# A three-stage kernel on one core: the first expert's routing, list and gather moved in the order of the work

## The chip, the cores and the metric

The kernel runs on one core of a Trainium2 chip, in one launch. The metric is the device time in microseconds (us). Five engines work side by side, each from its own queue in order: TensorE (PE), VectorE (DVE), ScalarE (ACT), GpSimd (POOL) and SyncE (SP, which only issues DMAs here). They meet at semaphores. An instruction that waits holds everything behind it in its queue.

## What is computed

Three stages, each fed by the one before, over N = 2304 tokens with 512 features:

```python
# 1 retention: 4 batches, 8 heads, 576 positions, head size 64
ret = scores * Dmat          # Dmat: gamma_h ** (i - j) for i >= j, else 0
x = (ret @ v) as [2304, 512]
# 2 experts: logits = x @ w_gate, [2304, 8]; the greedy assignment goes through
#   all (token, expert) pairs by falling logit, each expert takes 288 tokens at most
out[mask_e] = relu(x[mask_e] @ w1[e]) @ w2[e]      # w1: 512x1024, w2: 1024x512
# 3 gated layer: h = x @ w_in (512x2048); out = (h * tanh(softplus(h))) @ w_out
```

## The kernel before, in words

**Retention** (`attention`). The tokens are 18 tiles of 128. A loop over tiles issues loads, scaling, scores, the carried state, outputs and, one tile late, `turn`: it transposes the tile's result on TensorE, where the same matmuls give the eight logits of each token, sums these on DVE into `L` (L248) and stores the rows to `x_scratch` in HBM. The order on PE, DVE and POOL is the program's own.

**Routing** (`choices`, `reached`, `route`). The greedy assignment is done one expert at a time: find the expert that fills up first, and the threshold logit at which it does. `choices` makes, for each token, the best logit and its expert as a one-hot (five DVE instructions, L357 to L362, over a range of tiles). `reached` (L369) marks which of 63 thresholds a token's best logit reaches. TensorE sums these marks over all tokens into `pF`; DVE tests which experts are full (`sat`, L374), TensorE turns that into a digit (`pD`, L458). Six such steps (s = 0 to 5, L419 to L458) give the threshold. Then DVE marks the tokens over it and at it (`gt`, `eq`), counts them with scans and a matmul (`pP`, L482), and has each token's place in the expert's list (`pos`, L495 to L504). Two instructions (L501, L502) put the taken tokens into `dead`, and `widen` (L515, L516) closes the expert in `L` and in `open`, so that `choices` can be made for the next. In the kernel before, the first choices are made after the loop, in two batches: tiles 0 to 15, then 16 and 17.

**List, gather, weights.** `tokens` turns `pos` into a list: small DVE instructions (L579 to L589), two halves of one-hots (`ohb`, L595), two halves of nine matmuls on TensorE (`pI`, L603), a sum on DVE (`chosen`, L607). GpSimd then issues three indirect DMAs of 96 rows each (L615, `xg`), TensorE transposes the rows (L636), ACT and DVE split them into a rounded part and its remainder (`xh`, `xl`). `weights_of` reads the expert's number on SP (from `eid`, L533) and loads 8 units of 512 KB (L551; units 0 to 3 are w1, 4 to 7 are w2) into 5 stage buffers; ACT rounds each (`whi`, L565), POOL or DVE subtracts (`wlo`, L568). Each product is three matmuls (high by high, high by low, low by high): `mma` is the expert's first layer (8 outputs of 12 matmuls), `mmb` the second (L779).

**The planner** (`run_tasks`). From the routing on, the order on every engine is made when the program is built: each task is a generator that asks for an engine, a time in ns, the events it follows and a priority; the planner keeps a clock for each engine, adds a HOP of 200 between tasks, takes the task that can begin first, and holds one back if a more urgent one would begin before it ends. The lines of a task between two requests are issued when the request is granted. The planned times thus set only the order in each queue; on the chip each instruction waits for its semaphores. Costs that matter here: the sums after the marks 1600, a half of the list's matmuls 740, three gather issues 4900, the gather's landing `GATHER` = 10000 behind them, a weight unit's landing 2000 (`DMA_WAIT`) for units 0 and 1 and 8000 (`LATE`) for the others. Priorities: `eid` -2, the list -1, routing 0, products 2, weights 3; smaller is more urgent.

`warm` fills TensorE with matmuls on zeros (215 and a HOP each in the plan, L789) from the first list until expert 0's features are there. `narrow` starts once expert 0's first output is planned: it reads w_in and w_out (8-byte numbers), makes 4-byte numbers of them on ACT, DVE and POOL, and writes them back for the last stage; 32 pieces of 512 KB, the first three loaded by SP. `final_units` then loads them as units 64 to 79.

**Gated layer** (`tiles`, `hidden`, `gate`, `outer`): six tiles of 384 tokens, all weights kept in SBUF; the change doesn't touch it.

Of the kernel before, what the change touches and what calls it, by code (L numbers as in the profile page):

```python
# [13 lines left out]
ALU = mybir.AluOpType  # L14
# [7 lines left out]
E = 8  # L22
# [3 lines left out]
NT = N // P  # L26
HP = H // 2
WARM = 11
STRADDLE = (4, 13)

GB = 96
# [9 lines left out]
PE, DVE, POOL, ACT, SP = "pe", "dve", "pool", "act", "sp"  # L41
# [3 lines left out]
DMA_WAIT = 2000  # L45
LATE = 8000
GATHER = 10000
SCATTER = 3200
FIRST = 163
SECOND = 216  # L50
# [2 lines left out]
FIRST_UNITS = 2  # L53
# [75 lines left out]
class Kernel:  # L129
# [3 lines left out]
    def attention(self):  # L133
        tc, nc, a = self.tc, self.nc, self.a
# [7 lines left out]
        with ExitStack() as st:  # L142
# [130 lines left out]
            scale(0, nc.vector)  # L273
            scale(1, nc.gpsimd)
            scale(2, nc.gpsimd)
            for t in range(NT - 1):
                load(t + 3)
                scale(t + 3, nc.gpsimd)
                scores(t + 1)
                carried(t, Sb[seen[0] % 2])  # L280
                outputs(t)
                state(t)
                turn(t - 1)
                if t == 6:
                    self.routing_consts()
            t = NT - 1
            carried(t, Sb[seen[0] % 2])
            outputs(t)
            turn(t - 1)
            self.psum = lambda name, shape: ps.tile(shape, F32, name=name, tag="pS" if name == "pF" else "pA", bufs=1 if name == "pF" else 2)  # L290
            G = self.marks_of()
            self.chosen = self.rw.tile([GB, E, 3], I32, name="chosen", bufs=1)
            pF = self.psum("pF", [P, E])
            early, late = slice(0, t - 1), slice(t - 1, NT)
            choice = self.choices(early)
            self.reached(choice, G, early)
            turn(t)
            self.choices(late, choice)
            self.reached(choice, G, late)
# [49 lines left out]

    def choices(self, ts=slice(0, NT), into=None):  # L350

        pool, v, L = self.rw, self.nc.vector, self.L
# [6 lines left out]
        v.tensor_tensor(cand, L[:, ts], raw[:, :, None].to_broadcast(both), op=ALU.is_equal)  # L359
        v.tensor_tensor(cand, cand, self.rc[:, None, RC["prio"]].to_broadcast(both), op=ALU.mult)  # L360
        v.tensor_reduce(top, cand, AX.X, ALU.max)
        v.tensor_tensor(oh, cand, top[:, :, None].to_broadcast(both), op=ALU.is_equal)  # L362
        return into

    def reached(self, choice, G, ts):

# [10 lines left out]
    def route(self):  # L377
# [3 lines left out]
        tc, nc, L, rw = self.tc, self.nc, self.L, self.rw  # L381
        rc, ic, icp, v = self.rc, self.ic, self.at("ic", U32), self.nc.vector
        choice, sat = self.first_step
        at = Event(0)
        self.marks = set()
        for i in range(E):
# [102 lines left out]
            if i:  # L489
                self.widen(i, ohe)  # L490
                self.spawn(self.weights_of(junk, at, i))
                choice = yield from self.choose(i, at)
            at = yield DVE, 1600, [marked, at], 0
            pose = rw.tile([P, NT], F32, name="pose")
            v.scalar_tensor_tensor(pose, scan[:, 1], pP[:, 1:2], eq, op0=ALU.add, op1=ALU.mult)  # L495
            v.scalar_tensor_tensor(pos, scan[:, 0], pP[:, 0:1], gt, op0=ALU.add, op1=ALU.mult)
            fin = self.at("fin")
            v.scalar_tensor_tensor(fin, pose, CAP + 0.5, eq, op0=ALU.is_lt, op1=ALU.mult)
            if i == 0:
                self.spawn(self.weights_of(junk, at, i))  # L500
            v.tensor_tensor(self.dead, self.dead, gt, op=ALU.add)  # L501
            v.tensor_tensor(self.dead, self.dead, fin, op=ALU.add)  # L502
            v.tensor_tensor(pose, pose, fin, op=ALU.mult)
            v.tensor_tensor(pos, pos, pose, op=ALU.add)  # L504
            self.spawn(self.tokens(i, pos, at))
            if i == 0:
                at = yield DVE, 300, [at], 0
                self.widen(i, ohe)
                choice = yield from self.choose(i, at)

# [7 lines left out]
    def choose(self, i, at):  # L518
        if i == E - 2:
            return None  # L520
        yield DVE, 1750, [at], 0
        return self.choices()

    def weights_of(self, junk, at, i):

        nc, a, rw = self.nc, self.a, self.rw
        units = {}
        self.weights.append(units)
        n0 = len(self.weights) * 8 - 8
        at = yield DVE, 160, [at], EID  # L530
        eid = rw.tile([P, 1], I32, name="eid")
        with nc.allow_low_precision(reason="small integers"):
            nc.vector.tensor_reduce(eid, junk, AX.X, ALU.add)  # L533
        at = yield SP, 1000, [at, *([lambda: self.loaded.get(n0 - 1)] if n0 else [])], 0
        e = nc.sync.value_load(eid[0:1, 0:1], min_val=0, max_val=E - 1)
        for u in range(8):
            if u < 4:
                src = a["w1"][bass.ds(e, 1), :, u * 256:(u + 1) * 256]
            else:
                src = a["w2"][bass.ds(e, 1), (u - 4) * 256:(u - 3) * 256, :]  # L540
            yield from self.unit(n0 + u, src.rearrange("o (k p) c -> p (o k) c", p=P),
                                 DVE if n0 == 0 and u < 2 else None, units, 3,
                                 *([lambda: self.fetched] if n0 == 0 and u == FIRST_UNITS else []))

    def unit(self, n, src, eng, into, prio, *after):

        before = [lambda: self.loaded.get(n - 1)] if n else []
        place = [lambda: self.staged.get(n - STAGES)] if n >= STAGES else []
        at = yield SP, DMA_ISSUE, [*after, *before, *place], prio
        st = self.stage.tile([P, 1024], F32, name="st")  # L550
        self.nc.sync.dma_start(st.rearrange("p (k c) -> p k c", k=src.shape[1]), src)  # L551
        self.loaded[n] = at
        self.spawn(self.split_unit(n, st, self.arrival(524288, at, LATE if 1 < n < E * 8 else DMA_WAIT), eng, into, prio))

    def split_unit(self, n, st, at, eng, into, prio):

        before = [lambda: self.rounded.get(n - 1)] if n else []
        place = [lambda: self.freed[n - NRING] if len(self.freed) > n - NRING else None] if n >= NRING else []
        pool = self.ring
        if n >= E * 8 + NRING:  # L560
            yield None, 0, [lambda: Event(0) if self.extra else None], prio
            place, pool = [], self.extra
        hi = yield ACT, 1060, [at, *before, *place], prio
        dst = (pool.tile([P, 1024], F32R, name="whi"), pool.tile([P, 1024], F32R, name="wlo"))
        self.nc.scalar.copy(dst[0], st)  # L565
        self.rounded[n] = hi
        lo = yield ({POOL: 2480, DVE: 1240} if eng is None else eng), 1240, [hi], prio
        (self.nc.vector if lo.engine == DVE else self.nc.gpsimd).tensor_tensor(dst[1], st, dst[0].bitcast(F32), op=ALU.subtract)  # L568
        self.staged[n] = lo
        into[n - E * 8 if n >= E * 8 else n % 8] = (*dst, lo)  # L570

    def tokens(self, i, pos, at):

        nc, a, rw, v = self.nc, self.a, self.rw, self.nc.vector
        pr = TOKENS
# [19 lines left out]
            v.tensor_tensor(ohb[:, ts], bb[:, ts, None].to_broadcast([P, NT // 2, GB]), self.rc[:, None, RC["slot"]].to_broadcast([P, NT // 2, GB]), op=ALU.is_equal)  # L595
        pI = None
        for ts, made in zip(halves, ready):
            at = yield PE, 740, [made, side, *([] if pI is not None else [self.bank])], pr
            if pI is None:
                nI, pI = self.take_bank(f"pI{i}")  # L600
                pI = pI[:, :6]
            for t in range(ts.start, ts.stop):
                nc.tensor.matmul(pI, self.ohb[:, t * GB:t * GB + P], R[:, t].rearrange("p g c -> p (g c)"), start=(t == 0), stop=(t == NT - 1))  # L603
# [8 lines left out]
        self.fetched = at  # L612
        xg = self.fx.tile([GB, 3, DM], F32, name="xg", bufs=2)
        for j in range(3):
            nc.gpsimd.indirect_dma_start(out=xg[:, j], out_offset=None, in_=a["x"],  # L615
                                         in_offset=bass.IndirectOffsetOnAxis(ap=idx[:, j:j + 1], axis=0))
        at = Event(at.t + GATHER)
        if i > 1:
            yield None, 0, [lambda: self.layer1.get(i - 2)], pr
        xh = self.fx.tile([P, HP, CAP], F32R, name="xh", bufs=2)  # L620
# [497 lines left out]
```

## Time and profile before

| | |
|---|---|
| runs | median 807.48 us of 3 (805.46 to 808.31) |
| the profiled execution | 804.62 us |
| its span, first to last instruction | 802.9 us |
| mean granted TensorE clock | 0.977 |
| busy: PE, DVE, ACT, POOL | 751.5, 669.9, 413.0, 466.9 us |
| HBM read, written | 88.93 MB, 22.54 MB |

The execution lasts 1.7 us longer than its span. The retention ends near 84 us, the first expert's products begin at 125, the gated layer near 385. Busy shares are over the whole span; the stages have different limits, so they are read stage by stage. Matmuls are pipelined, and a busy PE is not PE at its peak.

### The profile page before, as it was taken

To read this page: it belongs to the slowest core of one execution; us is meant where nothing else is said; L and a number is where in the kernel's file an instruction comes from. 1 tells how busy PE (TensorE), PEld (TensorE's weight loads), DVE (VectorE), ACT (ScalarE), POOL (GpSimd) and SP (SyncE) were. 2 spreads that over 40 slices of the span, in tenths; PEclk is the share of its full clock that TensorE was granted. 3 is DMA by queue.
4 is the path that set the end of the run, shared out by engine and by line. 5 is a ranking of instruction groups with operands and counts; after the bars stand their busy time and mean duration, and the time that the engine had idled before them with its cause. 6 is when DMAs were issued, how large, how long until landed. Compare 5 with 4: busy or idle time off the path is not lost.

```text
span 802.9 us, 16174 instructions
## 1 busy us (share of the span) xinstructions
PE 751.5 (94%) x6184; PEld 678.4 (85%) x6184; DVE 669.9 (83%) x1089; ACT 413.0 (51%) x781; POOL 466.9 (58%) x406
## 2 busy tenths in 40 slices
PE   6999479998999999799999899999999999999996
PEld 4889338888898999799889799899988999899985
DVE  3444687888999988687798999989998998998993
ACT  1233115556556565666664555555556456555552
POOL 4643035779797797230176766656557556565644
PEclk9999679999999999899999999999999999999999
DMA  9993165788798888987500010001001001000001
GB/s 340 408 360 134 41 201 206 255 272 281 259 308 266 273 278 236 344 288 239 189 2 20 20 40 21 20 26 34 2 20 46 15 20 40 20 1 20 21 1 39
DMA packets 61261, 112.52 MB, mean 140 GB/s; under 512 B 4864, under 2 KB 33152, under 8 KB 61184
## 3 DMA queue, kind: packets, MB, share of 16 engines
q1 hardware_dynamic: 44960, 74.00, 27.3%
q10 hardware_dynamic: 13248, 28.06, 10.3%
q0 software_dynamic: 2976, 9.44, 3.6%
q8 instruction: 48, 0.79, 0.4%
q14 instruction: 29, 0.24, 0.1%
HBM read 88.93 MB, written 22.54 MB: 139 GB/s over the span
## 4 chain that ended last, share of the span: by engine, by line
PE 61%; DVE 24%; issue 5%; DMA 4%; ACT 2%; POOL 2%; SPq 0%; ACTq 0%; POOLq 0%; DVEq 0%
PE mmc L995 19%; PE po L1056 18%; PE mmb L779 7%; PE mma L779 5%; DVE q L1025 4%; DVE G L435 2%; DVE n L1020 2%; PE pX L246 2%; PE pT L232 2%; DMA qk<-qk 2%; PE pA L195 2%; DVE hl L805 2%; PE pF L453 2%; DVE ohb L595 2%; DMA st<-w 1%
## 5 line engine op out<-in xcount | busy, mean ns | idle before, releaser
L1025 DVE RECIPROCAL q<-q 128x384 f32<-128x384 f32 x96 | 244.3, 2545 | 11.4 <-ACT q L1016 5.6
L1027 POOL TENSOR_TENSOR n<-n,q 128x384 f32<-128x384 f32 x96 | 99.2, 1034 | 140.5 <-DVE q L1025 139.6
L1037 POOL TENSOR_TENSOR gl<-n,gh 128x384 fp32r<-128x384 f32 x96 | 105.3, 1097 | 50.8 <-ACT gh L1035 50.4
L995 PE MATMUL mmc<-yl,whi 128*128 128x384 f32 x384 | 130.2, 339 | 4.3 <-POOL yl L955 2.6
L995 PE MATMUL mmc<-yh,whi 128*128 128x384 f32 x384 | 130.0, 339 | 1.1 <-ACT yh L952 1.0
L995 PE MATMUL mmc<-yh,wlo 128*128 128x384 f32 x384 | 129.7, 338 | 0.0
L568 POOL TENSOR_TENSOR wlo<-st,whi 128x1024 fp32r<-128x1024 f32 x49 | 117.0, 2400 | 10.8 <-ACT whi L565 10.0
L1056 PE MATMUL po<-whi,gh 128*128 128x512 f32 x288 | 114.0, 396 | 0.0
L1056 PE MATMUL po<-whi,gl 128*128 128x512 f32 x288 | 113.9, 395 | 0.0
L1056 PE MATMUL po<-wlo,gh 128*128 128x512 f32 x288 | 113.3, 393 | 0.0
L1013 ACT ACTIVATE s<-mmc 128x384 f32<-128x384 f32 x96 | 47.2, 491 | 121.9 <-PE mmc L995 118.7
L1020 DVE SCALAR_TENSOR_TENSOR n<-s 128x384 f32<-128x384 f32 x96 | 103.2, 1075 | 2.1 <-ACT s L1013 1.2
L565 ACT CAST whi<-st 128x1024 fp32r<-128x1024 f32 x80 | 82.0, 1044 | 39.5 <-DMA st<-w 30.1
L995 PEld LDWEIGHTS mmc<-yl,whi 128*128 128x128 f32 x384 | 72.1, 188 | 9.5 <-POOL yl L955 3.5
L779 PE MATMUL mma<-xh,whi 128*128 128x288 f32 x256 | 77.0, 301 | 2.4 <-DVE xl L628 2.4
L779 PE MATMUL mmb<-hl,whi 128*128 128x288 f32 x256 | 78.1, 305 | 0.0
L779 PE MATMUL mmb<-hh,whi 128*128 128x288 f32 x256 | 77.7, 304 | 0.0
L779 PE MATMUL mmb<-hh,wlo 128*128 128x288 f32 x256 | 77.4, 302 | 0.0
L995 PEld LDWEIGHTS mmc<-yh,whi 128*128 128x128 f32 x384 | 72.2, 188 | 6.0 <-ACT yh L952 2.0
L779 PE MATMUL mma<-xh,wlo 128*128 128x288 f32 x256 | 76.7, 299 | 0.0
L779 PE MATMUL mma<-xl,whi 128*128 128x288 f32 x256 | 76.6, 299 | 0.0
L995 PEld LDWEIGHTS mmc<-yh,wlo 128*128 128x128 f32 x384 | 72.1, 188 | 0.0
(149 smaller groups left out, 1539.5 us busy)
## 6 DMA issues: line engine op xcount, KB each, us to landing
st<-w SPq DMA_DIRECT2D x64, 512.0 KB, 5.6
qk<-qk SPq DMA_DIRECT2D x18, 512.0 KB, 8.7
kv<-kv SPq DMA_DIRECT2D x18, 512.0 KB, 5.4
std<-w_out ACTq DMA_DIRECT2D x15, 512.0 KB, 5.3
std<-w_in ACTq DMA_DIRECT2D x14, 512.0 KB, 5.7
x_scratch<-xs SPq DMA_DIRECT2D x18, 256.0 KB, 4.7
y_scratch<-y ACTq DMA_DIRECT2D x32, 144.0 KB, 4.3
yt<-y_scratch SPq DMA_DIRECT2D x22, 192.0 KB, 2.4
```

What stands on the lines that cost most here:

```text
L195: nc.tensor.matmul(pA[i][o, hp, :], QK[t][sl, 1, hp, o], QK[t][sl, 0, hp, :], start=True, stop=True)
L232: nc.tensor.matmul(PT[t][q * 64:q * 64 + 64, i, k, :], KV[t][:, 1, 4 * k + 2 * q + i, :], AM[t][:, i, 2 * k + q, :], start=(first and k == ...
L565: self.nc.scalar.copy(dst[0], st)
L568: (self.nc.vector if lo.engine == DVE else self.nc.gpsimd).tensor_tensor(dst[1], st, dst[0].bitcast(F32), op=ALU.subtract)
L779: self.nc.tensor.matmul(bank[1][:, :CAP], al if h == 2 else ah, bl if h == 1 else bh, start=(first and j == h == 0), stop=(last and j == n ...
L995: self.nc.tensor.matmul(bank[1][:, :TILE], (wl if h == 2 else wh)[:, c, cs], x[c][h == 1], start=(c == h == 0), stop=(c == HP - 1 and h == 2))
L1013: nc.scalar.activation(s, p, AF.Sigmoid)
L1020: v.scalar_tensor_tensor(u, s, 2.0, s, op0=ALU.subtract, op1=ALU.mult)
L1025: v.reciprocal(q, q)
L1027: nc.gpsimd.tensor_tensor(u, u, q, op=ALU.mult)
L1037: nc.gpsimd.tensor_tensor(gl, u, gh.bitcast(F32), op=ALU.subtract)
L1056: nc.tensor.matmul(po[j], (gl if h == 2 else gh)[:, js], (wl if h == 1 else wh)[:, f % 2], start=(f == h == 0), stop=(f == DFF // P - 1 an ...
```

## The change

The first choices of tiles 0 to 8, 9 to 12 and 13 to 15 are made inside the retention loop, after the turn of the tile that completes them; only tiles 16 and 17 are left behind it. For expert 0 the place sums and the list's tasks come before the sums into `dead` and before `widen`, and its next choices are planned in two parts (650 and 1000 instead of one of 1750); some planned costs change with that. Expert 0's units 0 and 1 are subtracted on POOL behind the gather's issue instead of on DVE. Its unit 2, and with it on SP all that stand behind, waits on the chip until the third gather DMA has landed. In the plan that gather lands 3000 behind its issue, not 10000, and units 2 to 7 land after 2000 instead of 8000.

```diff
+EARLY = (9, 13, 16)
+GATHERED = 3000
+            G, choice = self.marks_of(), None
             for t in range(NT - 1):
...
+                if t in EARLY:
+                    ts = slice(max([0] + [e for e in EARLY if e < t]), t)
+                    choice = self.choices(ts, choice)
+                    self.reached(choice, G, ts)
...
-            early, late = slice(0, t - 1), slice(t - 1, NT)
-            choice = self.choices(early)
-            self.reached(choice, G, early)
+            late = slice(EARLY[-1], NT)
             turn(t)
             self.choices(late, choice)
             self.reached(choice, G, late)
...
-            at = yield DVE, 1600, [marked, at], 0
+            at = yield DVE, 1600 if i else 1250, [marked, at], 0
...
+            def buried():
+                v.tensor_tensor(self.dead, self.dead, gt, op=ALU.add)
+                v.tensor_tensor(self.dead, self.dead, fin, op=ALU.add)
+
+            if i:
+                buried()
+            v.tensor_tensor(pose, pose, fin, op=ALU.mult)
+            v.tensor_tensor(pos, pos, pose, op=ALU.add)
             if i == 0:
                 self.spawn(self.weights_of(junk, at, i))
-            v.tensor_tensor(self.dead, self.dead, gt, op=ALU.add)
-            v.tensor_tensor(self.dead, self.dead, fin, op=ALU.add)
-            v.tensor_tensor(pose, pose, fin, op=ALU.mult)
-            v.tensor_tensor(pos, pos, pose, op=ALU.add)
             self.spawn(self.tokens(i, pos, at))
             if i == 0:
-                at = yield DVE, 300, [at], 0
+                at = yield DVE, 650, [at], 0
+                buried()
                 self.widen(i, ohe)
                 choice = yield from self.choose(i, at)
...
-        yield DVE, 1750, [at], 0
-        return self.choices()
+        if i:
+            yield DVE, 1750, [at], 0
+            return self.choices()
+        at = yield DVE, 650, [at], 0
+        parts = self.choice_parts()
+        into = next(parts)
+        yield DVE, 1000, [at], 0
+        next(parts, None)
+        return into
...
-                                 DVE if n0 == 0 and u < 2 else None, units, 3,
-                                 *([lambda: self.fetched] if n0 == 0 and u == FIRST_UNITS else []))
+                                 POOL if n0 == 0 and u < FIRST_UNITS else None, units, 3,
+                                 *([lambda: self.fetched and Event(self.fetched.t + GATHERED)] if n0 == 0 and u == FIRST_UNITS else []))
...
+        if n == FIRST_UNITS:
+            self.tc.add_manual_dep(d.ins, self.gathering.name, mybir.DependencyInfo(mybir.DependencyClass.Sync, mybir.DependencyReason.DATA),
+                                   reason="the first expert's rows go ahead of its later weights")
...
-        self.spawn(self.split_unit(n, st, self.arrival(524288, at, LATE if 1 < n < E * 8 else DMA_WAIT), eng, into, prio))
+        self.spawn(self.split_unit(n, st, self.arrival(524288, at, LATE if E <= n < E * 8 else DMA_WAIT), eng, into, prio))
...
-        lo = yield ({POOL: 2480, DVE: 1240} if eng is None else eng), 1240, [hi], prio
+        lo = yield ({POOL: 2480, DVE: 1240} if eng is None else eng), 2480 if eng == POOL and n < E else 1240, [hi, *([lambda: self.fetched] if n < FIRST_UNITS else [])], prio
...
-            at = yield PE, 740, [made, side, *([] if pI is not None else [self.bank])], pr
+            at = yield PE, 740 if i else 480, [made, side, *([] if pI is not None else [self.bank])], pr
...
+        self.gathering = d.ins
+        at = Event(at.t + (GATHER if i else GATHERED))
-        at = Event(at.t + GATHER)
```

`choice_parts` is the former `choices` cut in two by a `yield` after the second of its five instructions; `choices` runs both parts.

## Rows read from the trace of the kernel before

**Rows 1.** Busy time by stage: window, PE, PEld, DVE, ACT, POOL, clock, DMA share, GB/s.

```profile
60.00:80.00 20.00, 20.00 (x437) 18.10 (x438) 9.44 (x20) 6.47 (x20) 7.13 (x7) 1.00 0.40 139
...
100.00:120.00 20.00, 14.56 (x134) 6.79 (x135) 16.84 (x61) 3.13 (x3) 6.14 (x4) 0.76 0.65 193
...
200.00:300.00 100.00, 96.41 (x1012) 91.80 (x1010) 91.13 (x288) 59.59 (x102) 83.57 (x49) 0.98 0.85 278
```

**Rows 2.** Timeline at the retention's end and in expert 0's search: start, length, engine, line.

```profile
82.11 2.12 PE L246 MATMUL pX<-both,xT 128*128 128x136 f32 x16
...
84.94 1.20 DVE L369 TENSOR_TENSOR G<-sc,rc 128x1008 bf16<-128x1008 f32 x1
86.06 0.17 DVE L248 TENSOR_REDUCE L<-pX 128x8 f32<-128x16 f32 x1
...
87.82 0.17 DVE L374 TENSOR_SCALAR sat<-pF 128x8 bf16<-128x8 f32 x1 [0.34 <-PE pF L301]
...
96.33 0.17 PE L458 MATMUL pD<-sat,digit 128*128 128x8 bf16 x1 [0.26 <-DVE sat L374]
```

**Rows 3.** Timeline of expert 0's list, DVE and PE.

```profile
103.41 5.13 PE L789 MATMUL warm<-idle,before 128*128 128x512 bf16 x13
...
104.39 0.17 DVE L501 TENSOR_TENSOR dead<-dead,sc 128x18 f32<-128x18 f32 x1
...
105.76 0.31 DVE L515 SCALAR_TENSOR_TENSOR L<-sc,L 128x144 f32<-128x144 f32 x1
...
106.63 2.02 DVE L595 TENSOR_TENSOR ohb<-sc,rc 128x864 bf16<-128x864 f32 x2
...
108.96 0.37 PE L603 MATMUL pI<-R,ohb 128*128 128x6 bf16 x9
...
110.29 0.15 DVE L607 TENSOR_REDUCE chosen<-pI 96x3 int32<-96x6 f32 x1
...
111.88 1.22 DVE L568 TENSOR_TENSOR wlo<-st,whi 128x1024 fp32r<-128x1024 f32 x1
```

**Rows 4.** Timeline of POOL: the gather of expert 0, a subtraction, expert 1's third issue.

```profile
110.72 1.11 POOL L615 DMA_INDIRECT xg<-x_scratch,chosen  x1 [39.50 <-DMA st<-w]
112.14 1.75 POOL L615 DMA_INDIRECT xg<-x_scratch,chosen  x1 [0.31 <-issue]
114.20 0.92 POOL L615 DMA_INDIRECT xg<-x_scratch,chosen  x1 [0.30 <-issue]
115.14 2.36 POOL L568 TENSOR_TENSOR wlo<-st,whi 128x1024 fp32r<-128x1024 f32 x1
...
145.92 0.92 POOL L615 DMA_INDIRECT xg<-x_scratch,chosen  x1 [0.30 <-issue]
```

**Rows 5.** DMA: queue 0 in 120 to 121, in 149 to 150; weight loads, issue to landing.

```profile
q0 software_dynamic: 51, 0.18, 56.8%
...
q0 software_dynamic: 16, 0.03, 9.3%
...
st<-w SPq DMA_DIRECT2D x64, 512.0 KB, 5.6
```

**Rows 6.** Timeline of PE: expert 0's first product, expert 1's transposes and first product.

```profile
125.12 0.38 PE L779 MATMUL mma<-xh,whi 128*128 128x288 f32 x1
...
157.41 1.15 PE L636 MATMUL mmx<-ident,xg 96*128 96x96 f32 x12
...
158.80 0.40 PE L779 MATMUL mma<-xh,whi 128*128 128x288 f32 x1
```

**Rows 7.** Timeline of DVE: the lists of experts 1 and 2.

```profile
143.06 0.15 DVE L607 TENSOR_REDUCE chosen<-pI 96x3 int32<-96x6 f32 x1
...
176.93 0.15 DVE L607 TENSOR_REDUCE chosen<-pI 96x3 int32<-96x6 f32 x1
```

**Rows 8.** Busy time and clock in 118 to 120, columns as in rows 1.

```profile
118.00:120.00 2.00, 2.00 (x24) 0.79 (x22) 1.37 (x6) 0.00 (x0) 0.00 (x0) 0.52 1.04 249
```

**Rows 9.** The chain that ended last, around experts 6 and 7: start, length, what.

```profile
319.58 11.38 DMA st<-w
```

More of the change, by code (lines that the diff above doesn't have):

```diff
@@ L290, in attention @@
             self.psum = lambda name, shape: ps.tile(shape, F32, name=name, tag="pS" if name == "pF" else "pA", bufs=1 if name == "pF" else 2)
-            G = self.marks_of()
             self.chosen = self.rw.tile([GB, E, 3], I32, name="chosen", bufs=1)
             pF = self.psum("pF", [P, E])
-            early, late = slice(0, t - 1), slice(t - 1, NT)
-            choice = self.choices(early)
-            self.reached(choice, G, early)
+            late = slice(EARLY[-1], NT)
             turn(t)
@@ L350, in choices, with choice_parts @@
     def choices(self, ts=slice(0, NT), into=None):
+        parts = self.choice_parts(ts, into)
+        into = next(parts)
+        next(parts, None)
+        return into
+    def choice_parts(self, ts=slice(0, NT), into=None):
         pool, v, L = self.rw, self.nc.vector, self.L
@@ L359, in choices @@
         v.tensor_tensor(cand, L[:, ts], raw[:, :, None].to_broadcast(both), op=ALU.is_equal)
+        yield into
         v.tensor_tensor(cand, cand, self.rc[:, None, RC["prio"]].to_broadcast(both), op=ALU.mult)
@@ L362, in choices @@
         v.tensor_tensor(oh, cand, top[:, :, None].to_broadcast(both), op=ALU.is_equal)
-        return into
     def reached(self, choice, G, ts):
@@ L520, in choose @@
             return None
-        yield DVE, 1750, [at], 0
-        return self.choices()
+        if i:
[3 more added lines that the diff above has]
+        parts = self.choice_parts()
+        into = next(parts)
+        yield DVE, 1000, [at], 0
+        next(parts, None)
+        return into
     def weights_of(self, junk, at, i):
@@ L550, in unit @@
         st = self.stage.tile([P, 1024], F32, name="st")
-        self.nc.sync.dma_start(st.rearrange("p (k c) -> p k c", k=src.shape[1]), src)
+        d = self.nc.sync.dma_start(st.rearrange("p (k c) -> p k c", k=src.shape[1]), src)
+        if n == FIRST_UNITS:
+            self.tc.add_manual_dep(d.ins, self.gathering.name, mybir.DependencyInfo(mybir.DependencyClass.Sync, mybir.DependencyReason.DATA),
+                                   reason="the first expert's rows go ahead of its later weights")
         self.loaded[n] = at
-        self.spawn(self.split_unit(n, st, self.arrival(524288, at, LATE if 1 < n < E * 8 else DMA_WAIT), eng, into, prio))
+        self.spawn(self.split_unit(n, st, self.arrival(524288, at, LATE if E <= n < E * 8 else DMA_WAIT), eng, into, prio))
     def split_unit(self, n, st, at, eng, into, prio):
@@ L614, in tokens @@
         for j in range(3):
-            nc.gpsimd.indirect_dma_start(out=xg[:, j], out_offset=None, in_=a["x"],
+            d = nc.gpsimd.indirect_dma_start(out=xg[:, j], out_offset=None, in_=a["x"],
                                          in_offset=bass.IndirectOffsetOnAxis(ap=idx[:, j:j + 1], axis=0))
-        at = Event(at.t + GATHER)
+        self.gathering = d.ins
+        at = Event(at.t + (GATHER if i else GATHERED))
         if i > 1:
```

## The prediction

> **What bounds the kernel now.** I read the stage table first, then the timeline at the seams of the stages, then the queues. The stage table [rows 1] shows the order of limits. In the retention (60 to 80 us) TensorE is busy all the time and VectorE for 9.44 of 20 us. Then the routing of the first expert is one chain of short VectorE and TensorE steps; the 14.56 us that TensorE shows from 100 to 120 are mostly fill (the warm matmuls). In 200 to 300 it is busy for 96.41 of 100 us beside a VectorE at 91.13: there products and routing share both engines. So what can be won lies between 82 and 125 us, where TensorE has no product to do, and the question is how much of a win there still stands when the full stretch begins.
>
> **The change, part by part.** *Early choices.* The last logits of the retention leave TensorE at 82.11 + 2.12 = 84.23, but VectorE reaches tile 17's sum only at 86.06, since the last write of the sixteen-tile batch runs up to 84.94 + 1.20 = 86.14, overlapping at its end [rows 2]. With tiles 0 to 15 chosen inside the loop, that sum can run at about 84.3: 1.8 us earlier, and with it the saturation at 87.82 and the whole single chain behind it. The batches moved in have 9, 4 and 3 tiles. The largest costs less than the one of sixteen, which can't begin before half of those turns is done (83.2) and so took under 3 us, some 1.7 in proportion; VectorE's free time in the loop is 20 - 9.44 = 10.6 us in each 20 [rows 1], about five tiles, so 2.1 us a tile, and the products of the mask it delays by some part of a us are used a tile later. I cost them at nothing; if that cover fails, each of three batches costs up to 1 us, 3 us in all. The third lies in a stretch where VectorE only waits.
>
> *First list ahead.* Before, between the marks and the list of tokens stand the two sums into dead (from 104.39) and the widening of L (105.76); behind the one-hots (106.63 + 2.02 = 108.65) stand expert 1's five choices, so the list, which TensorE has ready at 108.96 + 0.37 = 109.33, is read at 110.29 [rows 3]. All of these move behind. On VectorE that is 0.3 + 0.35 us ahead of the one-hots. But TensorE's first half of the list also waits for thirteen warm matmuls (103.41 + 5.13 = 108.54), which the planner lays out one per 415 ns of its own time (215 and a hop of 200). Its VectorE block before the list shrinks by 350 + 300 - 200 ns or so, that is by one matmul of 5.13/13 = 0.39 us. So TensorE ends the list 1.8 + 0.4 earlier, at 107.1, and the list is read at 107.2 instead of 110.29: 3.1 us earlier (3.7 if no warm matmul held it, 2.1 if as many are laid out as before). What moves behind delays expert 1's routing: it gains 3.1 less the 1.7 us or so of sums and choices now in front, 1.4, and gets back up to 2.4 where the two subtractions of 1.22 leave VectorE [rows 3]; I take 1.2 of that.
>
> *The gather.* Its three issues took 1.11, 1.75 and 0.92 us [rows 4]; the 1.75 fell beside a subtraction on VectorE [rows 3], and expert 1's issues show 0.92 with 0.30 between. I take three of 0.92: from 107.5 to 111.1, against 115.12. The landing: queue 0 still moved 0.18 MB in the microsecond before 121 [rows 5], some 6 us behind the last issue, with six weight units on the same engines; of expert 1's gather only 0.03 MB was left at 149 to 150, at most 3.2 us behind 145.92 + 0.92. With the later weights held back until it has landed, I take 2.6 (nothing below 1.5, since 0.2 MB a piece has to pass; 6 if the two first units disturb it as much as six did), 113.7. The transposes, which the planner now places 3000 ns behind the issue instead of 10000, go to about 114.1, and the first product, some 2 us behind them, from 125.12 to about 116.2 [rows 6]: 8.9 us.
>
> *What waits in its place.* On SP, unit 2's load holds units 3 to 7 and the three first loads of the narrowing. Unit 2 is asked for at 113.7 and needs its transfer (median 5.6 us, [rows 5]; alone on the engines perhaps 4), a rounding of 1 us on ACT and 2.4 us on GpSimd [rows 4]: ready at 121 to 123. Units 0 and 1 feed 48 matmuls, which at the pace of 0.13 us last until 122.6. It is about even, and later units need 2.4 us each on GpSimd against 3.2 us on TensorE. The first two subtractions, now on GpSimd behind the gather, end near 113.5 and 116; the second is first needed at 119.3. I cost these at nothing; if the cover goes, 1 to 3 us.
>
> *What is left at expert 1.* Expert 0's work now ends by about 148 to 150 instead of 158.8, but expert 1's transposes don't follow by 9 us. The planner still counts 10000 ns for that gather and so puts four steps of expert 2's search ahead of them on TensorE: they ran at 157.41, 14.35 us behind expert 1's list at 143.06 [rows 6, 7]. That list hangs on VectorE's chain, which now shares TensorE with products from 116 on. Between two lists there were 32.8 us with products for half of it and 33.9 with products throughout (143.06 to 176.93). Gains of 1.4 + 1.2 less 1.1 for that, and perhaps 1 of narrowing that now falls in earlier, leave the list near 142.5 (141 to 144.5). Behind it, four steps without products in front took 8.5 us in expert 0's search (87.82 to 96.33 [rows 2]); with products, 14.35. I take 10, since expert 0's products are through when they begin but narrowing isn't: 152.5, 4.9 us before 157.41. The ends are 149.5 (7.9 gained) and 158.9 (1.5 lost). Of the 4.9 I take off 0.9 for matmuls at half clock (below).
>
> **Sum.** From 1.8 (seam) + 1.3 (list) + 5.8 (gather and placement) = 8.9 us at the first product, 4.9 are left at the second expert and 4.0 behind the clock. From there on the order is nearly the old one and TensorE nearly full, so that these 4.0 go to the end: 804.62 - 4.0 = 800.6 against the profiled execution's own 804.62. This stands 2.86 below the median of the runs; so 807.48 - 4.0 = 803.5.
>
> **Rivals.**
> *The whole 8.9 us last.* For it: TensorE stands 96% busy later on, so work started sooner ends sooner. Against it: expert 1's list and its placement, as above. It needs the list near 139 and search steps without a wait. 807.5 - 8.5 = 799.
>
> [...]
>
> *Slower: the late weights of the last two experts.* The chain has one load of weights that took 11.38 us at 319.58 [rows 9], twice the usual, with TensorE waiting behind it. The planner lays all tasks out again once the first ones move, and that load's place behind the narrowing's loads may get worse. The gain of 4 is gone when it lands 4 us later against its neighbours; if the stall doubles, 11 - 4 = 7 us are lost, and half of that, with luck elsewhere, gives 811. Against it: gates (stage buffers, ring places) move together with the products, and each expert's requests keep their distance.
>
> *The change does not do what it says* only if the added wait on SP came too late to spare the gather; then the landing stays near 6 us behind the last issue, at 117, the first product at 119.5, and still earlier than the list of expert 1 allows: the same sum.
>
> **How the numbers follow.** A measurement of this kernel tells about 0.3%, 2.4 us, from no change. Forecast (2.5 to 6.5 us gained, 801 to 805): 0.48. All lasting: 0.14. The wait only moves: 0.26. Slower: 0.12. So faster 0.62, same 0.26, slower 0.12. Leaving out the far end of the slower case and some of the all-lasting one, the range is 798.5 to 809.
>
> **What would show it.** Right: the last logits' sum at 84.3, the list at 107 to 107.5, three issues of 0.92, queue 0 empty by 114, the first product at 116, expert 1's transposes near 152.5, and from there a constant lead of 4 to 5 us. Wrong: a transposition of expert 1 at 157 or later (the wait moved), or a lead that is there at 300 and gone at 335 (the late weights), or TensorE waiting for unit 2 between 119 and 124.

## The result and the profile after

The changed kernel is slower: 812.44 us median of 20 runs against 807.06 us of 20 runs of the kernel before, ratio 1.0072 (95% interval 1.0056 to 1.0088). The prediction was 803.5 us in a range of 798.5 to 809. The profiled execution took 810.29 us with a span of 808.5 us, 5.67 us above the one shown of before.

The early steps came as described. In the timeline of the changed kernel (start, length, engine, line), VectorE has the last logits' sum at 84.45 where [rows 2] had 86.06, list 0 at 107.67 (110.29 in [rows 3]), but list 1 at 143.24 and list 2 at 177.28 (143.06 and 176.93 in [rows 7]). The three lines on GpSimd answer to [rows 4], the products and transposes on TensorE to [rows 6]:

```profile
84.45 0.17 DVE L250 TENSOR_REDUCE L<-pX 128x8 f32<-128x16 f32 x1 [0.75 <-PE pX L248]
...
107.67 0.16 DVE L633 TENSOR_REDUCE chosen<-pI 96x3 int32<-96x6 f32 x1 [0.72 <-PE pI L629]
...
108.12 1.10 POOL L641 DMA_INDIRECT xg<-x_scratch,chosen  x1 [36.71 <-DVE sc L368]
109.53 0.92 POOL L641 DMA_INDIRECT xg<-x_scratch,chosen  x1 [0.30 <-issue]
110.76 0.92 POOL L641 DMA_INDIRECT xg<-x_scratch,chosen  x1 [0.30 <-issue]
...
114.89 1.64 PE L663 MATMUL mmx<-ident,xg 96*128 96x96 f32 x9
...
118.01 0.37 PE L806 MATMUL mma<-xh,whi 128*128 128x288 f32 x1 [0.26 <-ACT xh L653]
...
143.24 0.15 DVE L633 TENSOR_REDUCE chosen<-pI 96x3 int32<-96x6 f32 x1
...
156.84 0.64 PE L464 MATMUL pF<-oh,G 128*128 128x8 bf16 x18 [1.57 <-DVE known L451]
157.34 2.16 PE L663 MATMUL mmx<-ident,xg 96*128 96x96 f32 x12
...
177.28 0.15 DVE L633 TENSOR_REDUCE chosen<-pI 96x3 int32<-96x6 f32 x1
```

So 7.1 us were won at expert 0's first product, and all of it was gone at expert 1's transposes (157.41 before). The busy time by stage (window, PE, PEld, DVE, ACT, POOL, clock, DMA share, GB/s) shows where TensorE lost it. First the changed kernel, then three windows of the kernel before:

```profile
60.00:80.00 20.00, 20.00 (x437) 18.00 (x436) 10.55 (x26) 6.46 (x20) 7.32 (x7) 1.00 0.40 139
...
150.00:155.00 5.00, 2.20 (x43) 1.68 (x43) 3.46 (x13) 4.19 (x7) 4.37 (x4) 0.92 0.74 238
155.00:160.00 5.00, 3.32 (x35) 3.15 (x35) 4.20 (x13) 2.81 (x7) 5.00 (x3) 0.50 0.96 318
200.00:300.00 100.00, 94.22 (x1002) 89.20 (x1001) 89.53 (x284) 59.10 (x101) 82.38 (x48) 1.00 0.85 277
305.00:310.00 5.00, 3.17 (x25) 2.94 (x23) 4.49 (x7) 1.24 (x3) 4.53 (x2) 1.00 0.95 305
310.00:315.00 5.00, 3.43 (x29) 3.05 (x30) 3.62 (x14) 0.00 (x0) 0.94 (x1) 0.62 0.58 202
```

```profile
150.00:155.00 5.00, 4.76 (x64) 4.37 (x63) 3.94 (x13) 3.37 (x5) 4.18 (x4) 1.00 0.83 235
...
305.00:310.00 5.00, 4.42 (x49) 4.18 (x48) 4.17 (x13) 1.24 (x3) 4.14 (x3) 1.00 1.09 360
310.00:315.00 5.00, 4.53 (x48) 4.29 (x47) 4.80 (x14) 3.34 (x5) 2.79 (x3) 1.00 0.78 247
```

In the retention the moved batches cost nothing: TensorE is still busy for 20.00 of 20 us [rows 1], VectorE for 1.1 us more. Expert 0's products end early, and TensorE then idles for 2.8 of the 5 us from 150 and works at half clock (0.50 granted) in the next 5. And there is a second hole from 305 to 315: TensorE is idle there for 3.4 us, where before it was idle for 1.05. Lists 5, 6 and 7 were read at 278.43, 310.40 and 315.22 before, and at 280.59, 313.33 and 321.40 after: 2.2, 2.9 and 6.2 us later. The last expert's output then comes 5.4 us later. The chain that ended last passes through that hole at one small VectorE instruction:

```profile
306.37 3.22 DVE R L615
...
314.01 4.50 PE mma L806 x19
...
322.24 2.37 DVE wlo L594 x2
...
324.62 10.22 DMA st<-w
```

L615 writes 54 bf16 numbers per partition into `R`, the right side of the list's matmuls (L589 before). It takes 0.26 us in expert 0's list. Here it took 3.31. The timeline of VectorE, GpSimd and TensorE around it:

```profile
302.44 7.08 POOL L594 TENSOR_TENSOR wlo<-st,whi 128x1024 fp32r<-128x1024 f32 x3
...
303.45 0.17 DVE L511 TENSOR_TENSOR dead<-dead,sc 128x18 f32<-128x18 f32 x1
...
305.86 0.17 DVE L611 TENSOR_SCALAR g<-sc 128x18 f32<-128x18 f32 x1
...
306.15 0.22 DVE L614 TENSOR_TENSOR R<-g,sc 128x54 bf16<-128x54 f32 x1
306.28 3.31 DVE L615 TENSOR_SCALAR R<-g,rc 128x54 bf16<-128x54 f32 x1
309.50 1.04 DVE L621 TENSOR_TENSOR ohb<-sc,rc 128x864 bf16<-128x864 f32 x1
...
310.60 0.36 PE L629 MATMUL pI<-R,ohb 128*128 128x6 bf16 x8 [2.42 <-DVE ohb L621]
311.93 0.19 PE L629 MATMUL pI<-R,ohb 128*128 128x6 bf16 x1 [0.97 <-DVE ohb L621]
...
314.98 0.44 PE L806 MATMUL mma<-xh,whi 128*128 128x288 f32 x1
315.22 0.44 PE L806 MATMUL mma<-xl,whi 128*128 128x288 f32 x1
```

It ends (309.59) when a run of three GpSimd subtractions ends (309.52). The one-hots (L621) stand behind it on VectorE, the list's matmuls wait for these, and the products of expert 5 stand behind the list's matmuls on TensorE. So TensorE waits for 2.42 us and again for 0.97, then runs at the lower clock (0.50 granted over 312 to 317.8): a matmul begins every 0.24 us instead of every 0.13, up to 317.86.

In the kernel before, the same instruction was held too, but for less and elsewhere. Two of its four holds, each with the GpSimd run that it lies in:

```profile
236.15 4.74 POOL L568 TENSOR_TENSOR wlo<-st,whi 128x1024 fp32r<-128x1024 f32 x2
239.26 1.70 DVE L589 TENSOR_SCALAR R<-g,rc 128x54 bf16<-128x54 f32 x1
...
269.37 4.75 POOL L568 TENSOR_TENSOR wlo<-st,whi 128x1024 fp32r<-128x1024 f32 x2
272.50 1.68 DVE L589 TENSOR_SCALAR R<-g,rc 128x54 bf16<-128x54 f32 x1
```

Each ends 0.06 to 0.08 us after the end of the run. Summed over the eight lists, the time above 0.26 was 4.28 us before and 5.72 after; at expert 6 it was nothing before and 3.05 after, although GpSimd was working around that list in both (the last section shows how it got by). The rows show the wait, 3.31 us against 0.26, and that it was no wait for one subtraction only, which would have ended near 307.2 here. What held the instruction is shown in no row.

### The profile page after: what moved, and what is told of

It reads as the page before. It is cut to its first block, busy times and chain, and to the rows that moved or that the text cites. A ratio compares the mean times of both kernels' runs of the same rounds, so it can differ in the third digit from the quotient of the medians.

```text
span 808.5 us, 16151 instructions
## 1 busy us (share of the span) xinstructions
PE 752.6 (93%) x6170; PEld 680.9 (84%) x6170; DVE 668.2 (83%) x1098; ACT 414.3 (51%) x781; POOL 474.2 (59%) x409
## 4 chain that ended last, share of the span: by engine, by line
PE 54%; DVE 11%; POOL 2%; DMA 2%; issue 2%; ACT 2%; ACTq 0%; SPq 0%; POOLq 0%; DVEq 0%
PE mmc L1022 23%; PE po L1083 21%; PE mmb L806 5%; PE mma L806 4%; DVE q L1052 2%; DMA st<-w 1%; DVE G L446 1%; DVE hl L832 1%; DVE ohb L621 1%; DMA st<-w_out 1%; POOL n L1054 1%; DVE R L615 1%; PE pF L464 1%; DVE words L772 1%; DVE dw L775 1%
## 5 line engine op out<-in xcount | busy, mean ns | idle before, releaser
L594 POOL TENSOR_TENSOR wlo<-st,whi 128x1024 fp32r<-128x1024 f32 x52 | 124.2, 2407 | 5.3 <-ACT whi L591 3.9
```

## The experiments

All leave the computation whole. "Ratio" is to the kernel before on the same chip, with its 95% interval; "held" is the length of the `R` instruction at expert 6.

### Which part loses

The first pair takes the kernel before and adds the early choices alone, then the first list ahead as well.

```diff
+                if t in EARLY:
+                    choice = self.choices(ts, choice)
+                    self.reached(choice, G, ts)
...
+            if i:
+                buried()
...
+                at = yield DVE, 650, [at], 0
+                buried()
```

> The kernel before with the early choices alone. Nothing behind the retention is laid out anew, so all seams shift together. Placement theory (the lead of the whole change is lost because expert 1's transposes stand behind the fifth step of expert 2's search on TensorE): here that order is the old one and nothing is gained or lost by it; tile 17's sum comes 1.7 us earlier and expert 0's list too, and since all queues keep their order the end moves by -1.5 us (0 to -2). Rival (early batches hold up the retention): the last turn ends later than 82.1 + 2.1 by 1 us or more, and the end is the same or later.

> The kernel before with the early choices and the list ahead, but with the old gather (10000 in the plan, no wait on the loads, the first two subtractions on VectorE). Placement theory: the list is read near 107.7 as in the changed kernel, expert 1's transposes near 156 (1 us earlier than before), the end 0 to 2 us earlier than before: the loss sits in the gather's part. Rival (any new plan costs): the order of experts 6 and 7 comes out worse here too, and the end is 3 us or more later than before though the transposes of expert 1 are not.

Measured: early choices alone 804.84 us, ratio 0.9967 (0.9951 to 0.9983), with the last logits' sum at 84.84 in its profile. With the list ahead 807.68 us, 1.0008 (0.9984 to 1.0032). The early choices gain 2.2 us to the end by the medians (1.4 to 4.0 by the interval), and the list ahead takes this back.

Then the gather part alone on the kernel before: GpSimd subtractions for units 0 and 1, the wait on the chip, the planned 3000 and 2000.

```diff
+                                 POOL if n0 == 0 and u < FIRST_UNITS else None, units, 3,
...
+            self.tc.add_manual_dep(d.ins, self.gathering.name, mybir.DependencyInfo(mybir.DependencyClass.Sync, mybir.DependencyReason.DATA),
...
+        at = Event(at.t + (GATHER if i else GATHERED))
```

> The kernel before with the gather's part alone (first two subtractions on GpSimd, wait on the later loads, the plan's 3000 and 2000), without early choices and without the list ahead. If the loss sits in the gather's part: expert 1's list 1 to 3 us later than before although the first product is 5 us earlier, and the end 4 to 8 us later than before (the changed kernel's loss and the 2 to 3 us that the other parts give). If it sits in the combination: within 2 us of before.

Measured: 814.61 us, 1.0096 (1.0063 to 1.0128), held 3.27. The loss is in this part.

### Is it where expert 1's transposes stand?

My first theory was that the change would win if the plan also put expert 1's transposes sooner. The planned landing of expert 1's gather goes from 10000 to 5000, then that of all later ones.

```diff
-        at = Event(at.t + (GATHER if i else GATHERED))
+        at = Event(at.t + (GATHERED if i == 0 else 5000 if i == 1 else GATHER))
...
+        at = Event(at.t + (GATHERED if i == 0 else 5000))
```

> The changed kernel, with expert 1's gather planned to land 5000 instead of 10000 behind its issue, the others as they are. In the plan the transposes of expert 1 then stand behind the third step of expert 2's search instead of the fifth. Placement theory: the transposes run near 152 instead of 157.3, TensorE doesn't fall to half clock there, and expert 2's transposes come 4 us or more earlier than in the changed kernel; the end is 3 to 6 us earlier than the changed kernel's. Rival (expert 1's list is the bound, the search only fills the wait): transposes earlier, but expert 2's search and list as late as before, expert 2's transposes within 1.5 us of the changed kernel's, end within 2 us of it.

> The changed kernel with the gathers of all later experts planned to land after 5000. Placement theory: each expert's transposes move ahead of two steps of the next search, and the end is earlier than with expert 1's alone, 5 to 9 us earlier than the changed kernel's. Rival (the gathers really land near 6 to 8 us behind the issue because of the weights beside them): TensorE then waits for rows at experts 2 to 7, in a queue that holds the search behind them, and the end is as late as the changed kernel's or later.

Measured: 818.13 us, 1.0138 (1.0108 to 1.0169), held 3.22; and 808.96 us, 1.004 (1.0016 to 1.0064), held 0.35. The runs of the second lie between 807.09 and 814.32 us, but for one of 1835.68 that the ratio leaves out. In the first, expert 1's transposes did run 4.65 us sooner, at 152.69, yet list 2 came at 178.59 instead of 177.28; 1.25 us of that are a hold of the `R` instruction in that list, so without it list 2 would come at the same time and no sooner. The times at the end have the holds in them and decide nothing. Where no list is held (next part and the one behind it), the first product comes at 116.12, 123.65 or 125.13 and the ratios are 0.9984, 0.9970 and 0.9971. So the theory falls: products started sooner do not carry to the end.

### The held instruction

The rewrite makes the same numbers from the copy of the same constants that lies in PSUM, on the changed kernel and on the kernel before:

```diff
-        v.tensor_scalar(R[:, :, :, 1], g, self.rc[:, RC["base"]][:, NT:], None, op0=ALU.mult)
+        v.tensor_tensor(R[:, :, :, 1], g, self.at("base")[:, NT:, None].to_broadcast([P, NT, 3]), op=ALU.mult)
```

> The changed kernel with one VectorE instruction of each list (the second column of R, a tensor_scalar from SBUF to bf16 in SBUF) written as a tensor_tensor whose second operand lies in PSUM; the numbers are the same. Theory of the blocked instruction: in the changed kernel this instruction took 3.31 us at expert 6 while three subtractions ran on GpSimd without a pause, and 0.26 where GpSimd was idle; written so it takes 0.2 to 0.3 us at all eight lists, expert 6's list comes 3 us or more earlier against expert 5's, and the end moves by -3 to -6 us against the changed kernel, to 806 to 809. Rival (the 3.31 us is a wait for data that shows as execution, or the end is set by the late weights alone): the time is still lost beside it, the end within 1.5 us of the changed kernel's.

> The kernel before with the same one instruction rewritten. Its eight lists lost 4.3 us to it in all (0.6 to 1.4 us each at experts 2 to 5). Theory of the blocked instruction: the search chain sets the pace, so the lists of experts 3 to 6 come 1 to 4 us earlier and the end -1 to -4 us against before. Rival (late weights set the end): lists earlier, the end within 1 us of before.

Measured: 804.42 us, 0.9984 (0.9967 to 1.0001) for the changed kernel, and 802.88 us, 0.9971 (0.9950 to 0.9991) for the kernel before. The timeline of the changed kernel with the rewrite has the same run of three subtractions around the instruction, which now passes at once:

```profile
299.27 7.10 POOL L594 TENSOR_TENSOR wlo<-st,whi 128x1024 fp32r<-128x1024 f32 x3
...
303.16 0.22 DVE L615 TENSOR_TENSOR R<-g,sc 128x54 bf16<-128x54 f32 x1
303.28 1.05 DVE L621 TENSOR_TENSOR ohb<-sc,rc 128x864 bf16<-128x864 f32 x1
```

Its windows, with columns as above:

```profile
305.00:310.00 5.00, 4.54 (x48) 4.30 (x47) 4.54 (x17) 2.09 (x5) 3.65 (x4) 1.00 1.05 336
310.00:315.00 5.00, 4.57 (x49) 4.34 (x48) 4.54 (x7) 4.22 (x13) 2.24 (x3) 1.00 0.43 111
```

All eight take 0.21 to 0.22 us, the second hole is gone and the clock stays at 1.00 there. A wait for data is ruled out, since the rewritten instruction reads the same `g`. The rewrite changes both the form and the place of one operand; L611 above has the old form with its input in PSUM and took 0.17 us in the run that held L615, so the form alone does not cause the hold. Against the changed kernel's profile, list 5 comes 3.1 us sooner (277.45), list 6 6.6 (306.69), list 7 8.9 (312.53) and the last output 8.4. The rows add up to that: holds at experts 3 to 5 above 0.26, 0.40 + 0.83 + 1.44 = 2.7; expert 6, 3.05; and 2.2 more between lists 6 and 7, where the products ran at the lower clock; 7.9 in all, where the two profiled executions differ by 8.44 us. By the ratios to the kernel before, 1.0072 and 0.9984, it is 0.9%, some 7 us. So the loss goes with this instruction, or nearly all of it: with the rewrite in both kernels the change is still 1.5 us behind (804.42 against 802.88 us), but these intervals overlap.

### Why nothing was won with the loss gone

My second theory was that list 1 stays because expert 0's products and expert 1's search now run together. First the changed kernel with the old planned 10000 for expert 0's gather, then the rewritten one with the old 8000 for the weights as well:

```diff
-        at = Event(at.t + (GATHER if i else GATHERED))
+        at = Event(at.t + GATHER)
...
-        self.spawn(self.split_unit(n, st, self.arrival(524288, at, LATE if E <= n < E * 8 else DMA_WAIT), eng, into, prio))
+        self.spawn(self.split_unit(n, st, self.arrival(524288, at, LATE if 1 < n < E * 8 else DMA_WAIT), eng, into, prio))
```

> The changed kernel with expert 0's gather planned to land 10000 behind its issue again; the wait on the loads and the real gather stay. The order on TensorE is then the old one: three steps of expert 1's search stand ahead of expert 0's transposes. Theory of the shared search (products begun earlier only stretch expert 1's search, which sets the pace): expert 0's first product starts near 121 instead of 117, yet expert 1's list comes 1.5 to 3 us EARLIER than in the changed kernel (near 141) and the end is 2 to 6 us earlier than the changed kernel's. Rival (the wait on the loads costs): the list as late as in the changed kernel, or expert 0's products wait for weights, and the end stays within 1.5 us of the changed kernel's.

> The changed kernel with the rewrite, and with the planned costs of before for expert 0's gather (10000) and for the landing of units 2 to 7 (8000); the wait on the chip and the subtractions on GpSimd stay. If a search stretched by expert 0's transposes and products is why list 1 doesn't come earlier, search 1 has TensorE and VectorE for itself again here: steps s=0 to s=3 take 8 to 9.5 us instead of 12.5, list 1 is read at 139.5 to 141 instead of 142.6, and the whole gives about 0.994 of before. If it is the wait on the chip itself (weights later, ScalarE's queue held) that costs, list 1 stays at 142.5 or later and the time at 0.998 to 1.001.

Measured: 807.59 us, 1.0008 (0.9990 to 1.0025), held 0.26, list 1 at 145.63; and 804.74 us, 0.9970 (0.9946 to 0.9995), list 1 at 142.74. The steps s=0 to s=3 of expert 1's search did take 8.3 us in both, 12.5 in the changed kernel and 9.5 before. But step s=4 took 8.5 and 4.8 us, and the list came no sooner: expert 0's features cross the search there instead. In the first of the two VectorE waited 2.90 us for them, since ScalarE had three roundings of weights in front of them, the first of which waited 7.15 us for weights that the wait on the chip holds back. Where products do run beside the search, VectorE's queue shows how they stretch it. First the changed kernel with the rewrite, where `hl` waits for a product's activation and the search's next instruction (L451) stands behind it; then the one with the old 10000 (timelines of VectorE and ScalarE):

```profile
119.73 0.46 DVE L832 SCALAR_TENSOR_TENSOR hl<-mma,hh 128x288 fp32r<-128x288 f32 x1 [2.44 <-ACT hh L829]
120.11 0.14 DVE L451 TENSOR_TENSOR known<-known,sc 128x1 uint32<-128x1 uint32 x1
```

```profile
118.98 1.04 ACT L591 CAST whi<-st 128x1024 fp32r<-128x1024 f32 x1 [7.15 <-DMA st<-w]
...
124.15 1.29 ACT L653 CAST xh<-mmx 128x288 fp32r<-128x288 f32 x4
...
124.57 1.55 DVE L655 TENSOR_TENSOR xl<-mmx,xh 128x288 fp32r<-128x288 f32 x4 [2.90 <-ACT xh L653]
```

So half of the theory stands (the shared search is slower), and the other half, that a free search gives an earlier list, fell twice: expert 0's features cross the search at one place or another.

### What the wait on the chip does

The changed kernel without the added wait, its plan and its orders unchanged:

```diff
-        if n == FIRST_UNITS:
-            self.tc.add_manual_dep(d.ins, self.gathering.name, mybir.DependencyInfo(mybir.DependencyClass.Sync, mybir.DependencyReason.DATA),
-                                   reason="the first expert's rows go ahead of its later weights")
```

> The changed kernel without the added wait on the chip: same plan, same order on every engine, but unit 2's load goes out as soon as SP reaches it. If the wait is what lands the gather sooner, expert 0's transposes run later than 114.9, at 117 to 119, and the first product at 120 or later. If the landing comes from the shorter issues and the plan alone, the transposes stay near 115. The end is not set there by either theory, since the list of expert 6 and the three subtractions in front of it stay: 1.005 to 1.009 by the theory of the held instruction; a time near or below before (1.000) would say that the wait itself is the loss.

Measured: 817.90 us, 1.0139 (1.0107 to 1.0171), held 3.20; slower than either theory gave. The transposes waited for the rows until 117.80, 5.4 us behind the last issue (111.44 + 0.92), and list 1 came at 147.42, 4.2 later than with the wait:

```profile
111.44 0.92 POOL L638 DMA_INDIRECT xg<-x_scratch,chosen  x1 [0.30 <-issue]
...
117.80 1.25 PE L660 MATMUL mmx<-ident,xg 96*128 96x96 f32 x7 [0.54 <-DMA xg<-x_scratch,chosen]
```

With the wait, queue 0 was empty by 114, at most 2.3 us behind the last issue's end (111.68). The wait does what it says. The plan needs it: it puts the transposes ahead of the search's steps, so that a late landing is paid by list 1.

### The version that beats both

Early choices and the rewrite on the kernel before, without and with the list ahead:

```diff
+EARLY = (9, 13, 16)
...
+        v.tensor_tensor(R[:, :, :, 1], g, self.at("base")[:, NT:, None].to_broadcast([P, NT, 3]), op=ALU.mult)
```

> Early choices alone, with the one held VectorE instruction rewritten. If the two gains are in different places (the early choices at the head of the first chain, the rewrite in front of the later lists) they add: early alone was 0.9967 of before and the rewrite alone 0.9971, so 0.9938, 802.5 us where before gives 807.5; list 6 near 305.5, the last expert's output about 4.5 us earlier than before. If the chain behind the last lists is set by the late weights or by TensorE, the two don't add: 0.996 to 0.998. In either case it should be faster than the changed kernel with the rewrite (0.9984), if the gather part still costs something without the held instruction.

> Early choices and the first list ahead, old gather and old plan, with the held instruction rewritten: it differs from the one with early choices and the rewrite only by the list ahead. If the list ahead gains 1 us or more that lasts, 0.992 of before; if it adds nothing that lasts, as the pair without the rewrite says (0.9967 without, 1.0008 with), it is no better than early choices with the rewrite alone: 0.994 to 0.998.

Measured: 803.36 us, 0.9956 (0.9937 to 0.9975), and 805.54 us, 0.9977 (0.9958 to 0.9996). The first has the lowest ratio of all, and its interval lies below 1, though it overlaps that of the rewrite alone (0.9950 to 0.9991). The two gains (0.0033 and 0.0029) come to 0.0044, not to 0.0062, which its interval just reaches (0.0063); its list 6 is at 307.75, not at the 305.5 expected. The list ahead gains nothing, and it seems to cost something: 2.2 us by the medians here, where the intervals overlap, and 2.8 in the first pair, where they do not (up to 0.9983, from 0.9984).

All kernels without the rewrite, by the hold at expert 6: with 0.26 to 0.35 us the ratios are 0.9967, 1.0008, 1.0008 and 1.0040; with 3.20 to 3.31 they are 1.0072, 1.0096, 1.0138 and 1.0139. Each hold is that of the one profiled execution; whether all runs of a kernel have it is not shown (those of the changed kernel lie between 807.90 and 816.45 us).

## Why the prediction was wrong

**Early choices: right.** 84.45 forecast as 84.3, the cover in the retention held, and the gain lasts.

**List ahead and issues: right in size at the list.** List 0 at 107.67 (forecast 107.2), issues of 1.10, 0.92 and 0.92 with VectorE's subtractions gone from beside them. But the 1.3 us that the sum takes from the list did not last: early choices alone ended at 0.9967, with the list ahead at 1.0008.

**Gather: nearly right.** Queue 0 empty by 114 (forecast 113.7). The first product came at 118.01 instead of 116.2, since the last of the transposes ran only at 117.05.

**The wait in its place: right.** The later weights cost products nothing that shows; TensorE was busy for 1.99 of 2 us from 118. Their price appears only in another order, where ScalarE's queue stands behind them (2.90 us above).

**What is left at expert 1: this step failed.** I had four steps of expert 2's search in front of expert 1's transposes. Five sums of marks stand there: the fifth ends at 157.48, right where the transposes begin. And I took 10 us for the steps once the products are out of the way; they took as long as before, 14.2 us from list 1 to the fifth sum's end (14.3 before), although TensorE was busy for only 2.20 of the 5 us from 150 (4.76 before). The whole way from list 1 (143.24) to list 2 (177.28) lasts 34.0 us, 33.9 before. The list's forecast of 142.5 was near, but the price of sharing the search (1.1) was too small: s=0 to s=3 took 3 us more. So nothing was left where I had 4.9. No run shows the 0.9 us that the sum takes off for matmuls at half clock; in its place the changed kernel had a granted clock of 0.50 over 155 to 160, where it was 1.00 before, and expert 1's transposes took 2.16 us there instead of 1.15 [rows 6]. Ahead of expert 0's products its clock was 0.50 over 114 to 116, and over 118 to 120, where [rows 8] had 0.52, it was 1.00.

**"From there on the order is nearly the old one and TensorE nearly full, so that these 4.0 go to the end": this sentence failed twice over.** A TensorE that is 96% busy [rows 1] was not the pacemaker here, where the list of the next expert came no sooner: 4.65 us won at expert 1's transposes were gone one list later (178.59 for 177.28). And the order was not the old one. The gather part's new plan shifts what GpSimd does around expert 6's list, and a VectorE instruction for which the sum has no term was held there from 306.28 on, through the rest of one subtraction and the whole of the next (3.05 us, and TensorE's granted clock fell after it, from 1.00 over 305 to 310 to 0.62 over 310 to 315). How the moment matters is shown in the last section.

The rival on the slower side had its place near the right experts, but not its mechanism: it named the late weights of the last two experts (11.38 us in [rows 9]), and that load took 10.22 after. The holds were there to be read in the kernel before, as an instruction with 0.26 us in one list and 1.70 in another.

**The 2.2 us by which list 5 is late.** Of these, 1.65 arise between lists 3 and 4 (212.49 to 247.37, where before it was 211.96 to 245.19). There two VectorE instructions of the narrowing (`words`) wait for ScalarE, and the next steps of expert 4's search stand behind them. First the changed kernel, then one of the kernel before, where none waits in that stretch:

```profile
222.01 0.76 DVE L772 TENSOR_SCALAR words<-words,ic 128x512 uint32<-128x512 uint32 x1 [0.83 <-ACT words L770]
...
227.64 0.76 DVE L772 TENSOR_SCALAR words<-words,ic 128x512 uint32<-128x512 uint32 x1 [0.85 <-ACT words L770]
```

```profile
224.38 0.75 DVE L745 TENSOR_SCALAR words<-words,ic 128x512 uint32<-128x512 uint32 x1
```

Both kernels that add the list ahead to the early choices have two such waits there, 1.67 and 1.62 us in all, and neither kernel with the early choices but without the list ahead has any; the kernel with the gather part alone has two as well (2.75 us). So the order was not the old one here either, and this is a likely price of planning anew, the list ahead included; no run took it away to prove it.

**What stays open.** No row accounts for the other 0.5 us of list 5: the holds of experts 3 to 5 were even smaller (2.7 against 3.7). The rewrite's profile has that list 1.0 us ahead of before, which shows the sum and not the path.

## What to carry to other kernels

Before counting on a busy engine to carry a gain to the end, find the chain that releases its work from one round to the next, and ask whether that chain got shorter. In a timeline, look for one instruction with several durations at the same shape: here its spread, 0.26 to 1.70 us before, showed a wait, and under the new order the longest was 3.31. One rewritten instruction (0.9971) was worth more than the whole rearrangement (1.0072).

## What the hardware showed that I had not expected

A VectorE instruction of 54 elements per partition was held through more than one GpSimd subtraction. The run of three began at 302.44 with 2.36 us each, so its second ended near 307.16. The waiting instruction had been there since 306.28 and did not get in at this seam between the second and the third; it ended at 309.59. In three more kernels it was held for 3.20 to 3.27 us, again longer than the 2.4 us of one subtraction. But it was not held every time. In the kernel before, at expert 6, and in the kernel with all later gathers at 5000 (the last two lines), it came 0.1 and 0.3 us ahead of such a seam and was through in 0.26 and 0.35 us, with GpSimd's next instructions right behind:

```profile
303.10 2.41 POOL L568 TENSOR_TENSOR wlo<-st,whi 128x1024 fp32r<-128x1024 f32 x1 [1.27 <-ACT whi L565]
305.46 1.34 POOL L762 TENSOR_TENSOR dw<-dw,dt 128x512 f32<-128x512 f32 x1
...
305.40 0.26 DVE L589 TENSOR_SCALAR R<-g,rc 128x54 bf16<-128x54 f32 x1
```

```profile
300.49 7.12 POOL L594 TENSOR_TENSOR wlo<-st,whi 128x1024 fp32r<-128x1024 f32 x3
...
304.97 0.35 DVE L615 TENSOR_SCALAR R<-g,rc 128x54 bf16<-128x54 f32 x1
```

So, by these rows, a queue of GpSimd work cost nothing or 3 us, depending on the moment at which the instruction comes; what decides at the seam is not shown. VectorE instructions with an operand in PSUM passed in the changed kernel's run: L511, with `sc` in PSUM, took 0.17 us at 303.45.

After 2.42 and 0.97 us of waiting, TensorE ran at half clock while it was working again (0.62 granted over 310 to 315, 0.50 over 312 to 317.8): matmuls 0.24 us apart until 317.86. So a hold of 3.05 us cost over 5: from list 5 to list 7 the changed kernel took 40.8 us, with the rewrite 35.1.
